# Moving three pieces of side work in a cached-attention training step: broadcast rows made earlier, a weight's transposes begun later, the last column sums put behind the attention rows

## The chip, the cores and the metric

The kernel runs on one core of one Trainium2 chip. The metric is the device time of an execution in microseconds (us). Executions of one kernel scatter by some 0.3%, so versions are compared on the same chip in alternating rounds. A ratio here is the mean time of one kernel's fast runs over that of the other's of the same rounds, so it is not quite the ratio of the medians that are quoted beside it. Times with two decimals such as 721.31 are read in a trace, counted from the start of its span.

## The reference, cut to what matters

```python
# x: 4 rows of 512; k_cache, v_cache: 4 x 32 heads x 4096 x 128 (bf16, 1 MB a head)
h   = x + attention(layernorm(x), k_cache, v_cache, wq, wo)
out = h + swiglu(layernorm(h), w1, w3, w2)
outputs: out, and the gradients to x, k_cache, v_cache, wq, wo, w1, w3, w2
```

There are 128 heads of 1 MB. The forward pass reads K and V once (256 MB). The backward pass reads V once more and writes one gradient of K and one of V per head: 3 MB a head, 384 MB. A head's 1 MB is 2^20 bytes, so these 640 MB are 671 of the 707.87 MB (of 10^6 bytes) that the profile counts; most of the rest are weights and their gradients.

## The kernel before

The forward pass forms, per head, P x K (`PK`), M = V' x PK on TensorE, and column sums of PK (`kP`). All arrays of a head live in 23 buffers of 1 MB. At the end of the forward pass come the attention rows, the norm and the MLP for four tokens, and from there dO, the gradient of the attention's output. Names that end in _ps or begin with pt_ are tiles that TensorE writes: al_ps takes the last attention rows, kt_ps the flushed sums, pt_hT the transposed rows for the norm, rb_ps the norm's mean and scale. A unit of wo is 8 transposes on TensorE and a copy.

```python
def M_end(s):                       # head s of the forward pass
    ...
    for c in range(2):
        for q in range(4):          # 8 matmuls: column sums of P x K into kP
            nc.tensor.matmul(hold["kP"][...], lhsT=ones_window(w), rhs=PK[...], ...)
    nc.scalar.copy(out=M_of(s), in_=hold["M"][:, 0:Dh + 1])
    PKs.pop(s).give(); Vs.pop(s).give()      # the buffers come free
# ... end of the forward pass
M_mm(NH - 1, 0, SJ); M_end(NH - 1)
O_cols(NH - MC, NH)
attn_page(2); attn_page(3)          # attention rows of the last pages
kP_flush(NH - 1)                    # ScalarE copy, 4 matmuls kt_ps, ScalarE copy
# ... norm, MLP, dO, first gv
```

The backward pass, per head: `V_T` transposes V (TensorE, evicted by ScalarE), 32 small matmuls make dP, which also frees V's buffer for a later load; VectorE writes the outer products gv (needs broadcast rows of dO) and gk (rows of q), and each goes out as one store of 1 MB.

```python
def front(s):
    if s % REP == 0:                # REP = 4: rows of dO and q for heads s..s+3
        replicate(s)                # 2 x (4 matmuls, ScalarE copy)
    V_T(s, psT)
    dP_ps = ...                     # 32 matmuls
    (vring if len(V2s) + len(VTs) + len(vring) < NV2 else free).append(sl.i)   # NV2 = 7

O0, S0 = 2, 21
for s in range(NH):
    prefetch()                      # loads of V into buffers of vring
    front(s + 1)
    grad_V(s + 1)                   # gv: VectorE, then its store
    grad_K(s)                       # gk
    if s >= S0:   step("s", 1 if s < S0 + 38 else 3)   # other gradients
    elif s >= O0: step("o")         # pages 1 to 3 of wo: transposes, then dO's columns and rows
```

## Time and profile before

| what | value |
|---|---|
| time, three runs | 1723.05 us median (1722.40 to 1723.24) |
| span of the profiled execution | 1719.8 us |
| bytes moved, mean rate | 707.87 MB, 412 GB/s |
| busy: TensorE, VectorE, ScalarE, GpSimd | 77%, 73%, 56%, 26% |
| busy: 16 DMA engines | 90% or more in 39 of 40 slices |

Read the row of DMA shares before the engines' shares. Where the transfers are busy from end to end, an engine's idle time has a price only if it leaves the transfers without work. The execution with this profile took 1721.68 us.

### The profile page before, as it was taken

To read this page: it belongs to the slowest core of one execution; us is meant where nothing else is said; L and a number is where in the kernel's file an instruction comes from. 1 tells how busy PE (TensorE), PEld (TensorE's weight loads), DVE (VectorE), ACT (ScalarE), POOL (GpSimd) and SP (SyncE) were. 2 spreads that over 40 slices of the span, in tenths; PEclk is the share of its full clock that TensorE was granted. 3 is DMA by queue.
4 is the path that set the end of the run, shared out by engine and by line. 5 is a ranking of instruction groups with operands and counts; after the bars stand their busy time and mean duration, and the time that the engine had idled before them with its cause. 6 is when DMAs were issued, how large, how long until landed. Compare 5 with 4: busy or idle time off the path is not lost.

```text
span 1719.8 us, 44279 instructions
## 1 busy us (share of the span) xinstructions
PE 1328.0 (77%) x19124; PEld 1124.5 (65%) x19124; DVE 1255.4 (73%) x1389; ACT 960.1 (56%) x1470; POOL 450.7 (26%) x808
## 2 busy tenths in 40 slices
PE   5888888888888888887787888767638777887771
PEld 4667666676666666876677877766536555665660
DVE  5989899889998997666667666766566566656582
ACT  3455444444454444677655555547537666766760
POOL 1211222222222231221233233322232332222221
PEclk9999999999999999666655555557765575555655
DMA  9999999999999999999999999999999999999997
GB/s 398 418 419 418 419 418 419 418 418 417 416 416 406 418 405 391 380 418 418 414 412 414 412 415 413 415 419 418 421 423 413 418 418 414 414 418 420 409 419 314
DMA packets 101867, 707.87 MB, mean 412 GB/s; under 512 B 11284, under 2 KB 15392, under 8 KB 17704
## 3 DMA queue, kind: packets, MB, share of 16 engines
q1 hardware_dynamic: 62272, 422.60, 59.4%
q0 software_dynamic: 39008, 282.37, 40.2%
q8 instruction: 150, 2.46, 0.6%
q14 instruction: 45, 0.37, 0.1%
q10 hardware_dynamic: 392, 0.07, 0.0%
HBM read 422.59 MB, written 282.34 MB: 410 GB/s over the span
## 4 chain that ended last, share of the span: by engine, by line
DMA 50%; PE 4%; DVE 3%; ACT 2%; issue 2%; POOL 0%; POOLq 0%; DVEq 0%; ACTq 0%
DMA out_dram<-gk 33%; DMA out_dram<-gv 15%; DMA out_dram<-gw 2%; ACT V L761 2%; DVE gk L766 1%; DVE gv L766 1%; PE pt_tps L760 1%; PE M_ps L433 1%; DVE PK L418 1%; PE pt_w L562 0%; PE gps L942 0%; ACT Pn L397 0%; PE kP_ps L443 0%; PE dP_ps L1148 0%; PE gu_ps L833 0%
## 5 line engine op out<-in xcount | busy, mean ns | idle before, releaser
L761 ACT COPY V<-pt_tps 128x1024 bf16<-128x1024 bf16 x512 | 492.5, 1016 | 192.0 <-PE pt_tps L760 131.8
L760 PE MATMUL pt_tps<-ident_b,V 128*128 128x128 bf16 x4096 | 453.2, 293 | 57.7 <-ACT V L761 53.7
L760 PEld LDWEIGHTS <-V 128*128 128x128 bf16 x4096 | 401.7, 138 | 122.3 <-issue 114.4
L766 DVE TENSOR_TENSOR gv<-P,reps 128x4096 bf16<-128x4096 bf16 x125 | 286.6, 2293 | 203.8 <-DMA out_dram<-gk 76.1
L766 DVE TENSOR_TENSOR gk<-dS,reps 128x4096 bf16<-128x4096 bf16 x128 | 293.4, 2292 | 108.5 <-DMA out_dram<-gv 54.3
L433 PE MATMUL M_ps<-PK,Vn 128*128 128x130 bf16 x4096 | 285.4, 222 | 50.6 <-DMA Vn<-in_A_v_cache_dram 50.2
L418 DVE TENSOR_TENSOR PK<-Kn,PK 128x4096 bf16<-128x4096 bf16 x128 | 292.3, 2284 | 32.3 <-POOL PK L414 32.0
L433 PEld LDWEIGHTS <-Vn 128*128 128x128 bf16 x4096 | 252.1, 99 | 72.0 <-DMA Vn<-in_A_v_cache_dram 66.3
L325 DVE STREAM_TRANSPOSE KT<-Kn 128x512 f32<-128x512 f32 (+1 forms) x321 | 250.7, 797 | 0.3 <-issue 0.2
L320 ACT COPY KT<-pt_tps 128x1024 bf16<-128x1024 bf16 x128 | 129.5, 1012 | 189.8 <-PE pt_tps L319 147.1
L1148 PE MATMUL dP_ps<-dOT_bf,V 128*128 128x1 bf16 x4096 | 145.4, 166 | 107.4 <-DVE dSt L1158 60.5
L1148 PEld LDWEIGHTS <-V 128*128 128x128 bf16 x4096 | 138.8, 104 | 122.4 <-issue 66.7
L1165 POOL DMA_DIRECT2D out_dram<-gk x128 | 68.2, 533 | 401.2 <-DMA out_dram<-gk 153.6
L331 POOL TENSOR_TENSOR W<-qrep,wmask 128x128 bf16<-128x128 bf16 x128 | 124.3, 971 | 81.8 <-PE S_ps L351 67.1
L414 POOL COPY PK<-P_all 128x64 bf16<-128x64 bf16 x128 | 32.6, 255 | 420.9 <-ACT P_all L408 417.8
L777 POOL DMA_DIRECT2D out_dram<-gv x128 | 68.4, 534 | 268.2 <-DMA out_dram<-gv 90.3
L1138 POOL COPY P<-P_all 128x64 bf16<-128x64 bf16 x125 | 127.4, 1019 | 0.0
L408 ACT COPY P_all<-pt_P 32x64 bf16<-32x64 bf16 x256 | 52.1, 203 | 59.5 <-PE pt_P L404 57.3
L319 PE MATMUL pt_tps<-ident_b,Kn 128*128 128x128 bf16 x1024 | 80.7, 223 | 0.0
L443 PE MATMUL kP_ps<-PK,onesw 128*32 128x512 bf16 x1024 | 79.2, 386 | 0.0
L319 PEld LDWEIGHTS <-Kn 128*128 128x128 bf16 x1024 | 62.1, 100 | 25.8 <-issue 25.8
L351 PE MATMUL S_ps<-KT,W 128*32 128x256 bf16 x1536 | 75.2, 285 | 0.5 <-DVE KT L325 0.2
(237 smaller groups left out, 1314.4 us busy)
## 6 DMA issues: line engine op xcount, KB each, us to landing
Kn<-in_A_k_cache_dram SPq DMA_DIRECT2D x128, 1024.0 KB, 15.6
Vn<-in_A_v_cache_dram SPq DMA_DIRECT2D x128, 1024.0 KB, 15.8
V<-in_A_v_cache_dram SPq DMA_DIRECT2D x128, 1024.0 KB, 10.9
out_dram<-gv POOLq DMA_DIRECT2D x128, 1024.0 KB, 27.4
out_dram<-gk POOLq DMA_DIRECT2D x128, 1024.0 KB, 27.3
wq<-in_A_wq_dram SPq DMA_DIRECT2D x8, 1024.0 KB, 10.3
out_dram<-gw POOLq DMA_DIRECT2D x6, 896.0 KB, 28.0
wo<-in_A_wo_dram SPq DMA_DIRECT2D x4, 1024.0 KB, 13.3
```

The source lines that it names most:

```text
L319: nc.tensor.transpose(pt[:, i, :], Kn[:, c * GW + i, :], ident_b[:])
L320: nc.scalar.copy(out=KT[:, c * GW:(c + 1) * GW, :], in_=pt[:])
L325: nc.vector.transpose(out=KT[:, c * w_:(c + n) * w_], in_=Kn[:, c * w_:(c + n) * w_])
L331: nc.gpsimd.tensor_tensor(out=W[:, hl], in0=qrep[:, :, s:s + 1].to_broadcast([P, 4, 32]), in1=wmask[:, hl, None, :].to_broadcast([P, 4, 32 ...
L418: nc.vector.tensor_tensor(out=PK[:, :, 0:Dh].rearrange("p j (r t) -> p j r t", t=2), in0=Ks[s].heads().rearrange("p j (r t) -> p j r t", t=2),
L433: nc.tensor.matmul(hold["M"][:], lhsT=Vn[:, j, :], rhs=PK[:, j, :], start=(j == 0), stop=(j == SJ - 1))
L443: nc.tensor.matmul(hold["kP"][32 * q:32 * (q + 1), :, :], lhsT=ones_window(w), rhs=PK[:, j0:j0 + 4, 0:Dh], start=(w == 0 and c == 0), stop ...
L760: nc.tensor.transpose(pt[:, i, :], v[:, g * GW + i, :], ident_b[:])
L761: nc.scalar.copy(out=v[:, g * GW:(g + 1) * GW, :], in_=pt[:])
L766: nc.vector.tensor_tensor(out=dst.rearrange("p j (r t) -> p j r t", t=2), in0=col2[:, :, None, :].to_broadcast([P, SJ, Dh // 2, 2]), in1=r ...
L1138: nc.gpsimd.tensor_copy(out=P2s[s][:], in_=P_all[:, s, :, None].to_broadcast([P, SJ, 2]))
L1148: nc.tensor.matmul(dP_ps[:, j:j + 1], lhsT=VT[:, j, :], rhs=dOT_bf[:, s:s + 1], start=True, stop=True)
```

## The change

Its intent: no wait for broadcast rows at the start of the backward pass, less side work for TensorE and ScalarE in its first heads, and a shorter way from the last head of the forward pass to the first store.

```diff
-    def M_end(s):
+    def kP_mm(s):                    # the 8 matmuls of the column sums
 ...
+        PKs.pop(s).give()
+
+    def M_end(s, kP=True):
+        if kP:
+            kP_mm(s)
 ...
-    M_end(NH - 1)
+    M_end(NH - 1, False)
 ...
     attn_page(3)
+    kP_mm(NH - 1)
     kP_flush(NH - 1)
 ...
-        woT(2, "s")                  # two units of wo before rb_ps
+        woT(1, "s")
 ...
         nc.tensor.matmul(rb_ps[:], lhsT=ones_f[0:B, :], rhs=rdiag[:], ...)
+        woT(1, "s")
 ...
-            if s % REP == 0:
-                replicate(s)
+            if s % REP == REP - 2 and s + 2 < NH:
+                replicate(s + 2)
 ...
-        O0, S0 = 2, 21
+        O0, S0 = 5, 24
 ...
-                step("s", 1 if s < S0 + 38 else 3)
+                step("s", 1 if s < S0 + 32 else 3)
```

More of the change, by code (lines that the diff above doesn't have):

```diff
@@ L447, in M_end @@
         nc.scalar.copy(out=M_of(s), in_=hold["M"][:, 0:Dh + 1])
-        PKs.pop(s).give()
         Vs.pop(s).give()
```

## The prediction

> **What bounds the kernel now.** I read the page's slices first, then the transfers' rate by stage, then the order of time around the few places where that rate is low.
>
> The row of DMA busy shares and the row of rates in the page (40 equal slices of the 1719.8 us span):
>
> ```profile
> DMA  9999999999999999999999999999999999999997
> GB/s 398 418 419 418 419 418 419 418 418 417 416 416 406 418 405 391 380 418 418 414 412 414 412 415 413 415 419 418 421 423 413 418 418 414 414 418 420 409 419 314
> ```
>
> The 16 DMA engines are busy in every slice, while no compute engine passes 77% (TensorE) over the span. The rate sits on a plateau of about 418 GB/s. The kernel moves 707.87 MB; at 418 GB/s this is 1693.5 us, so only 26 us of the span are not explained by bytes at the plateau. The table by stage says where they are (columns: stretch, its length, busy time and count of PE, PEld, DVE, ACT, POOL, then granted clock, DMA share, GB/s):
>
> ```profile
> 0.00:4.00 4.00, 0.00 (x0) 0.00 (x0) 0.84 (x6) 1.28 (x1) 2.76 (x17) 1.00 0.55 166
> 4.00:662.00 658.00, 547.35 (x9103) 449.26 (x9104) 588.81 (x795) 321.17 (x708) 164.87 (x384) 0.99 1.01 417
> 662.00:680.00 18.00, 16.21 (x241) 12.41 (x243) 10.29 (x10) 5.96 (x15) 2.23 (x3) 1.00 1.05 356
> 680.00:702.00 22.00, 20.84 (x395) 18.40 (x387) 10.81 (x34) 13.15 (x20) 0.58 (x3) 0.84 1.02 415
> 702.00:714.00 12.00, 10.44 (x148) 9.60 (x149) 9.09 (x16) 7.59 (x10) 4.47 (x7) 0.67 0.95 381
> 714.00:730.00 16.00, 12.36 (x188) 11.04 (x186) 11.15 (x9) 11.24 (x13) 4.04 (x7) 0.61 0.92 345
> 730.00:1702.00 972.00, 720.77 (x9061) 623.82 (x9059) 624.44 (x524) 599.72 (x706) 271.72 (x391) 0.60 1.01 416
> 1702.00:1719.80 17.80, 0.00 (x0) 0.00 (x0) 0.00 (x0) 0.00 (x0) 0.00 (x0) 0.50 0.40 169
> ```
>
> A stage loses length x (418 - rate) / 418: 2.4 us at the start, 1.6 in the forward pass, 2.7 in 662-680, 0.2 in 680-702, 1.1 in 702-714, 2.8 in 714-730, 4.7 in 730-1702, 10.6 in the drain: 26 in all. In 662-680 the engines are full (share 1.05); there the packets are short (wo arrives in 1 KB pieces: 2,408 of 2,546 packets in 662-672 are under 2 KB). The change touches neither the start, nor these packets, nor the bytes. What it can reach is the hand-over to the backward pass, 702-730: 1.1 + 2.8 = 3.9 us, or 0.23%.
>
> **What the Trainium skill says.** "DMA: Bandwidth & Descriptors", section "Where 436 GB/s comes from", puts the ceiling of the 16 ports at 435 GB/s; the plateau of 418 is 96% of it, so I take it as the wall. The same page, "Anatomy of one DMA", fits a transfer as 2.0 us plus bytes over 436 GB/s: 4.4 us for 1 MB. The trace has 4.7 us for the gv store issued at 717.95 with little beside it, which agrees, and 27.4 us for the median store: the rest is queueing behind other transfers. "Perfetto Trace Analysis", "Identifying the Most-Contended Engine", says to improve that engine first; here this is the transfers, and nothing in the diff shortens one.
>
> **Part 1: rows two heads ahead (and part 2, wo later).** Before, the broadcast rows of dO and q for heads 4 to 7 are made at the front of head 4, in TensorE's and ScalarE's way, behind the first wo unit. In order of time (start, length, what, idle before and who ended it; lines of other engines cut):
>
> ```profile
> 725.83 0.37 PE L1148 MATMUL dP_ps<-dOT_bf,V 128*128 128x1 bf16 x8 [0.49 <-ACT V L761]
> ...
> 726.06 1.01 PE L571 MATMUL pt_wo<-ident_b,wo 128*128 128x128 bf16 x8
> ...
> 727.12 1.01 ACT L215 COPY wo<-pt_wo 128x1024 bf16<-128x1024 bf16 x1 [1.34 <-PE pt_wo L571]
> 728.02 0.59 ACT L1129 CAST reps<-rep_ps 128x512 bf16<-128x512 f32 x1
> ...
> 728.70 2.29 DVE L766 TENSOR_TENSOR gv<-P,reps 128x4096 bf16<-128x4096 bf16 x1 [3.30 <-ACT reps L1129]
> ```
>
> VectorE stood 3.30 us for those rows. In the changed kernel they come at the front of head 2: gv(4) can follow gk(2) directly, 2.4 us earlier than 728.70, and gk(3), gv(5) likewise. The buffer it needs is free: only four output buffers rotate here, gv(4) takes that of gv(2), landed by 717.95 + 4.7 = 722.7.
>
> But the work only moves. Two sets of four small matmuls with ScalarE copies of 0.59 us take TensorE from 727.01 to 729.18, 2.2 us. Set before the transposes of head 2 (now at 715.69), they push dP(2) from 721.2 to 723.4 and dP(3) from 726.2 to 728.4. dP(2) releases the buffer for the load of V issued at 721.31, and dP(3) that at 726.27: both loads start 2.2 us later. gk(2), 723.11 before, slips by some 0.8 us. The third load (734.81) comes about 1.4 us earlier, because wo units cost heads 2 to 4 each about 0.9 us of TensorE and 1.01 us of ScalarE, which are now spent after head 5.
>
> What is this worth in transfers? From 714 to 721 only stores are in flight, and their times do not change (gk(0) issued 713.42, gv(2) 717.95, gk(1) 720.75): the 0.70 and 0.72 shares of 716-720, loss 1.2 us, stay. From 722 to 728 the share is already 0.93 to 1.07 with rates of 283 to 360, loss 1.4 us. There the late loads cost up to 0.5 us (one transfer fewer in flight around 722-724) and the stores that come 2.4 us sooner give back up to all of 1.4. I estimate a gain of 0.9, between 0 and 1.4. From 728 on the rate is 418 again and an earlier store only queues longer. The rows are also waited for at five later places (7.5, 7.5, 2.0, 11.5 and 6.3 us of VectorE, between 1306 and 1478). They will vanish, but the transfers run at 414 to 416 GB/s with share 1.01 there: worth nothing. Side work begins at head 24 instead of 21 but takes triple steps from 56 instead of 59, so its some 207 steps end at head 114 instead of 115: no change.
>
> **Part 3: the last column sums and the wo unit.** In order of time before:
>
> ```profile
> 679.81 0.62 PE L443 MATMUL kP_ps<-PK,onesw 128*32 128x512 bf16 x8
> ...
> 681.12 1.89 PE L478 MATMUL al_ps<-wo,OT_bf 128*4 128x512 bf16 x8
> ...
> 684.05 0.19 ACT L458 COPY kPT<-kt_ps 128x32 f32<-128x32 f32 x1 [2.99 <-PE kt_ps L457]
> 684.29 0.41 PE L806 MATMUL pt_hT<-ident_f,rows_t 4*128 4x4 f32 x4 [0.28 <-ACT kPT L458]
> ...
> 685.63 0.38 PE L820 MATMUL rb_ps<-rdiag,ones_f 4*128 4x8 f32 x2
> ```
>
> The eight sums (0.55 us net) leave their place before the attention rows, which end at 682.5 instead of 683.0. But the flush of the sums still stands before pt_hT in TensorE's order. Before, its ScalarE copy (0.59) lay beside the attention rows; now it cannot start before the sums, at 683.0: copy to 683.6, kt_ps (1.02) to 684.7, its copy to 685.0, pt_hT at 685.0 instead of 684.29. ScalarE's square root for the norm also queues behind that copy (684.85 becomes about 685.0). One wo unit (0.5 us) before rb_ps instead of two wins 0.5 back, the other fills the gap of 0.68 us before gu_ps. Net, rb_ps at about 685.9 instead of 685.63: I expect the first store of gv to come 0.2 us LATER, not earlier. As 702-714 waits on it, this costs 0.2.
>
> **Sum.** 1723.05 - 0.9 + 0.2 = 1722.35; I go to 1722.0, since the late waits on rows that vanish may give the transfers a little in the 414 GB/s stretches.
>
> **Rivals.** (a) The hand-over closes wholly: -3.9, so about 1719. For it: the 3.30 us wait stands exactly in the low-rate stretch. Against: half of the loss lies before 722, on stores that the change does not move. (b) Held buffers starve the stores: pages 1 to 3 of wo keep their three buffers three heads longer, so four outputs rotate to head 10 instead of 7. With four, 760-840 ran at 417 GB/s and share 1.01 (four rising to six), so I give it nothing; were the share there 0.95 for three heads of 7.5 us, it would cost 1.1 us: 1723.5. (c) The path before the first gv grows by 0.7 us, pt_hT's whole slip: 1722.9. (d) The drain: 10.6 us of loss after 1702 depend on how evenly the last stores (3.0 MB are left at 1702) lie over the 16 engines; shifts upstream can move it by 2 us either way, unrelated to the intent.
>
> **Range and chances.** The mechanisms span about -3.9 to +1.8; with the drain's scatter and the 0.8 us between the three runs, 1717.5 to 1726.0 should hold it. A change of 2% is 34 us; all loss that is not bytes is 26, so faster by 2% is nearly excluded. Slower by 2% needs a starved backward pass, for which the trace gives no sign.
>
> **What would show it.** Right: bytes and plateau unchanged; no wait of gv on the rows; loads of V issued near 723.5 and 728.4 by this clock; pt_hT near 685.0; 714-730 at 350 to 385 GB/s instead of 345. Wrong: 730-850 under 410 GB/s or share under 0.98 (buffers starve, b); 716-720 filled (a); gv(0) issued earlier than 707.79 (part 3 misread); a drain of much over or under 18 us (d).

## The result, and the profile after

The changed kernel took 1725.80 us median (1724.54 to 1728.72, six runs) against 1723.14 (1722.40 to 1724.24, six runs): ratio 1.0016, 95% interval 1.0003 to 1.0029. This lies in the stated range and within 2%, but on the other side of zero from the point that was forecast. Two later comparisons, on chips 14 and 5, gave 1.0003 (0.9989 to 1.0017) and 1.0002 (0.9989 to 1.0015).

The table by stage of the kernel after, with the columns of the prediction's table:

```profile
662.00:680.00 18.00, 16.19 (x255) 12.35 (x246) 10.94 (x10) 5.87 (x14) 2.49 (x4) 1.00 1.06 363
680.00:702.00 22.00, 20.63 (x369) 17.81 (x367) 10.48 (x32) 13.00 (x19) 0.50 (x3) 0.84 1.02 415
702.00:714.00 12.00, 9.82 (x185) 9.10 (x183) 8.69 (x17) 6.54 (x9) 3.05 (x5) 0.85 0.90 358
714.00:730.00 16.00, 13.08 (x190) 11.75 (x188) 13.20 (x12) 11.35 (x13) 9.34 (x11) 0.58 0.95 371
730.00:1702.00 972.00, 733.61 (x9070) 637.12 (x9066) 623.09 (x522) 600.86 (x707) 270.12 (x391) 0.58 1.01 416
1702.00:1723.40 21.40, 0.00 (x0) 0.00 (x0) 0.00 (x0) 0.00 (x0) 0.00 (x0) 0.50 0.34 144
```

Apart from 662-680 (363 GB/s instead of 356, ahead of the change), three rows differ from before. 702-714 fell from 381 to 358 GB/s: the first store of gv comes later. Its issue before,

```profile
707.79 0.63 POOL L777 DMA_DIRECT2D out_dram<-gv  x1 [3.88 <-DVE dOT_bf L735]
```

and after:

```profile
709.35 0.63 POOL L782 DMA_DIRECT2D out_dram<-gv  x1 [3.82 <-DVE dOT_bf L740]
```

714-730 rose from 345 to 371, as forecast, though mostly for another reason than the one forecast (see the point on the late loads below). And the drain after 1702, when only stores are left, is 3.6 us longer, at 144 GB/s instead of 169.

The chain of instructions at the end of the forward pass, in order of time (start, length, engine and instruction; other rows cut):

```profile
681.60 1.46 PE L482 MATMUL al_ps<-wo,OT_bf 128*4 128x512 bf16 x6
...
682.68 0.40 PE L443 MATMUL kP_ps<-PK,onesw 128*32 128x512 bf16 x3
682.89 0.38 PE L482 MATMUL al_ps<-wo,OT_bf 128*4 128x512 bf16 x1
...
683.11 0.38 PE L482 MATMUL al_ps<-wo,OT_bf 128*4 128x512 bf16 x1
...
683.98 0.58 ACT L458 COPY kP_sb<-kP_ps 128x512 f32<-128x512 f32 x1 [2.87 <-PE al_ps L482]
...
685.97 0.41 PE L811 MATMUL pt_hT<-ident_f,rows_t 4*128 4x4 f32 x4 [0.28 <-ACT kPT L462]
...
687.15 0.59 PE L825 MATMUL rb_ps<-rdiag,ones_f 4*128 4x8 f32 x2
```

The sums' copy on ScalarE (683.98), which lay beside the attention rows before, now follows them and holds up pt_hT. The sums' matmuls also slip in ahead of the last two of the attention rows, although they stand behind them in the program; all five traces with the sums moved show the same order.

The heads 2 to 4 of the backward pass, in order of time:

```profile
716.92 0.60 PE L1132 MATMUL rep_ps<-dOrows_bf,ident_b 32*128 32x128 bf16 x4
...
722.60 0.83 PE L1154 MATMUL dP_ps<-dOT_bf,V 128*128 128x1 bf16 x24
...
724.88 2.29 DVE L771 TENSOR_TENSOR gk<-dS,reps 128x4096 bf16<-128x4096 bf16 x1
...
727.08 2.29 DVE L771 TENSOR_TENSOR gv<-P,reps 128x4096 bf16<-128x4096 bf16 x1
```

gv(4) starts at 727.08 directly after gk(2), with no wait on rows; before, it started at 728.70 after a wait of 3.30 us. No wait of gv on the rows' copy is left anywhere in the trace; before there were six, 38.1 us in all. But dP(2), which starts at 722.60, releases the first load of V. The load queue before,

```profile
721.31 0.33 SPq L793 DMA_DIRECT2D V<-in_A_v_cache_dram  x1
...
726.27 0.33 SPq L793 DMA_DIRECT2D V<-in_A_v_cache_dram  x1
```

and after:

```profile
724.37 0.33 SPq L798 DMA_DIRECT2D V<-in_A_v_cache_dram  x1
...
729.72 0.33 SPq L798 DMA_DIRECT2D V<-in_A_v_cache_dram  x1
```

Both loads start 3.1 to 3.5 us later. Of this 0.9 us is the forward pass, which ran that much later in this execution (the last block of M began at 678.77 instead of 677.84, in code that the change does not touch); the rest, 2.1 to 2.5 us, is the change, about the 2.2 us of the prediction. There is a stretch of low rate behind them. In windows of 2 us of the kernel after:

```profile
732.00:734.00 2.00, 1.76 (x35) 1.61 (x32) 2.00 (x2) 1.81 (x3) 1.18 (x2) 0.50 1.00 360
734.00:736.00 2.00, 1.75 (x23) 1.75 (x24) 1.14 (x3) 0.61 (x2) 1.36 (x2) 0.50 0.98 279
```

Before, the same two windows ran at 442 and 410 GB/s, while 724-728 ran at 283 and 328. The DMA engines count as busy there; it is the packets that take longer. The transfers of the last of these windows by queue (packets, MB, share of the 16 engines):

```profile
q1 hardware_dynamic: 63, 0.52, 93.1%
```

93.1% of 16 engines for 2 us is 29.8 us, or 473 ns for each of 63 load packets, with hardly a store beside them. In the traces a packet of 8 KB in the stores of the drain takes 309 ns (median). But loads that run alone are not slow as such. In the same trace the stores were slow at 726-728 (453 ns each), and at 728-730 the loads ran just as alone at 317 ns each and 389 GB/s. The queue of the stores in the first of these windows and that of the loads in the second:

```profile
q0 software_dynamic: 61, 0.40, 86.3%
...
q1 hardware_dynamic: 94, 0.77, 93.0%
```

Why packets take longer in some of these windows stays open.

### The profile page after: what moved, and what is told of

The parts are those of the page before. It is cut to its first block, busy times and chain, and to the rows that moved or that the text cites. A ratio compares the mean times of both kernels' runs of the same rounds, so it can differ in the third digit from the quotient of the medians.

```text
span 1723.4 us, 44279 instructions
## 1 busy us (share of the span) xinstructions
PE 1341.0 (78%) x19124; PEld 1138.7 (66%) x19124; DVE 1255.3 (73%) x1389; ACT 959.7 (56%) x1470; POOL 450.9 (26%) x808
## 4 chain that ended last, share of the span: by engine, by line
DMA 48%; PE 4%; DVE 4%; ACT 3%; issue 2%; POOL 1%; POOLq 0%; DVEq 0%; ACTq 0%
DMA out_dram<-gk 34%; DMA out_dram<-gv 12%; DVE gk L771 2%; ACT V L766 2%; DMA out_dram<-gw 1%; DVE gv L771 1%; PE pt_tps L765 1%; PE M_ps L433 1%; DVE PK L418 1%; PE gps L948 0%; POOL P L1144 0%; PE pt_w L566 0%; ACT Pn L397 0%; PE dP_ps L1154 0%; PE kP_ps L443 0%
## 5 line engine op out<-in xcount | busy, mean ns | idle before, releaser
L765 PE MATMUL pt_tps<-ident_b,V 128*128 128x128 bf16 x4096 | 460.6, 296 | 58.8 <-ACT V L766 54.3
L765 PEld LDWEIGHTS <-V 128*128 128x128 bf16 x4096 | 408.5, 140 | 131.7 <-issue 123.8
L771 DVE TENSOR_TENSOR gv<-P,reps 128x4096 bf16<-128x4096 bf16 x125 | 286.6, 2293 | 200.1 <-DMA out_dram<-gk 92.3
L418 DVE TENSOR_TENSOR PK<-Kn,PK 128x4096 bf16<-128x4096 bf16 x128 | 292.3, 2284 | 33.4 <-POOL PK L414 33.1
L1154 PEld LDWEIGHTS <-V 128*128 128x128 bf16 x4096 | 139.5, 104 | 109.7 <-ACT V L766 59.7
L397 ACT ACTIVATE Pn<-E,rl 128x1024 bf16<-128x1024 f32 x64 | 73.7, 1152 | 3.2 <-DVE rl L394 3.2
```

The source lines that it names most:

```text
L418: nc.vector.tensor_tensor(out=PK[:, :, 0:Dh].rearrange("p j (r t) -> p j r t", t=2), in0=Ks[s].heads().rearrange("p j (r t) -> p j r t", t=2),
L765: nc.tensor.transpose(pt[:, i, :], v[:, g * GW + i, :], ident_b[:])
L771: nc.vector.tensor_tensor(out=dst.rearrange("p j (r t) -> p j r t", t=2), in0=col2[:, :, None, :].to_broadcast([P, SJ, Dh // 2, 2]), in1=r ...
L1154: nc.tensor.matmul(dP_ps[:, j:j + 1], lhsT=VT[:, j, :], rhs=dOT_bf[:, s:s + 1], start=True, stop=True)
```

## The experiments

Twelve runs were made: the changed kernel twice more (e1, e8) and ten other kernels. Bytes moved up to a moment are worked out from the trace of each; with transfers never short of work, 0.42 MB are 1 us.

**The change once more (e1) and a third time (e8).** No edit.

> The changed kernel once more, beside its parts on the same chip. It measured 1.0016 of before. All theories: 1.0010 to 1.0025 again, about +2.7 us. Its trace tells whether the late end of the transfers repeats: in the first trace 21.4 us after 1702 at 144 GB/s, against 17.8 us at 169 GB/s before. Theory T (the loss is in the hand-over, through the longer path to the first gv): 702-714 again near 358 GB/s and gv(0) about 1.5 us later than before. Rival D (the end of the run is uneven over the DMA engines, which has nothing to do with the intent): the stretches up to 1702 are level with before and the extra time lies after it.

> The changed kernel a third time, since the first comparison gave 1.0016 (1.0003 to 1.0029) and the second 1.0003 (0.9989 to 1.0017). If there is a real loss: 1.0005 to 1.0015. If the first was chance: 0.9993 to 1.0008. Bytes moved at 1690 us again 699.8 to 700.0 MB, as in every trace so far; what differs is the thinning of the engines after that.

Measured: e1 1724.42 us median against 1724.17 of before (ratio 1.0003, 0.9989 to 1.0017); e8 1723.96 against 1724.78 (1.0002, 0.9989 to 1.0015). At 702-714 e1 ran at 367 GB/s, and its drain was long again (21.5 us after 1702). In e8 699.60 MB had moved at 1690 us, under the 699.8 that were forecast. The loss of the first comparison did not repeat: 0.3 to 0.5 us in place of 2.7, none of it told from zero.

**Each part alone.**

```diff
 e2: +            if s % REP == REP - 2 and s + 2 < NH: replicate(s + 2)
 e3: +        O0, S0 = 5, 24        (and S0 + 32)
 e4: +    kP_mm(NH - 1) behind attn_page(3);  woT(1) on both sides of rb_ps
```

> Only the rows of dO and q two heads ahead; wo from head 2 and the sums as before. Prediction's step: -0.9 us (0 to -1.4), ratio 0.9992 to 1.0000. Rival B (held wo buffers cost): exactly before, 1.0000, as wo is not touched. Rival D: anything within 2 us of before, and no relation to 714-730 in its trace.

> Only pages 1 to 3 of wo begun at head 5 instead of 2, side work at 24 instead of 21. Theory T: -0.5 to 0 us. Rival B (three buffers held three heads longer starve the stores): +2 to +3 us, ratio 1.0012 to 1.0018, nearly the whole loss, and a rate under 410 GB/s between 750 and 850. Rival D: within 2 us either way, rates up to 1700 as before.

> Only the last column sums behind the attention rows and one of two wo units moved behind rb_ps. Prediction's step: +0.2 us; the trace of the changed kernel shows the way from the last M to the first gv longer by 0.63 us, so theory T now says +0.6 us, ratio 1.0003. If the hand-over carried the whole loss it would be +2.7 us, 1.0016. Rival B: 1.0000.

Measured against the same runs of before (1724.17 us median): e2 1723.50, ratio 0.9997 (0.9984 to 1.0009); e3 1724.01, 1.0003 (0.9991 to 1.0016); e4 1724.24, 1.0004 (0.9991 to 1.0016). None is told from zero. The interval of e3 still allows the smaller losses that rival B named, but its trace shows no starving: from 760 to 900 us, with the buffers held, it moved 58.4 MB (before: 58.0). In the trace of e2 alone the loss in 714-730 even grew (316 GB/s): of the 0.45 MB missing against before, 0.34 are missing at 726-730. The first load had come at 723.29 and the wo units still delayed the heads after it; that these are the cause is not shown.

**A dose of delay (e5, e6).** Does a microsecond that the transfers lose in the hand-over cost a microsecond at the end? I doubted it after seeing how unevenly the 16 engines finish.

```diff
+        for _ in range(16):          # e6: 48
+            nc.vector.tensor_copy(out=u[:], in_=u[:])
         nc.vector.tensor_tensor(out=dhT[:], in0=u[:], in1=grT[:], op=ALU.add)
```

> The kernel before with 16 copies of u onto itself put into VectorE's chain just before dO's rows, so that the first gv and all stores after it come some 3.3 us later (16 x 0.21 us, the step between such operations in the trace). A dose of the loss that the change was to remove. Theory T (time lost by the transfers in the hand-over is lost at the end): 730 us into the span about 1.3 MB behind before (300.35 MB), and +3.3 us at the end, ratio 1.0019. Theory S (the end is set by the one or two DMA engines that lag; the gap is a gap of those that run ahead, and is made up later): as far behind at 730, but the difference shrinks by 1118, and the end moves by 0 to 1.5 us, ratio 1.0000 to 1.0009.

> The same with 48 copies, 10 us. Theory T: +10 us, ratio 1.0058, and 4 MB behind at 730 as well as at 1690. Theory S: more than the lag of the slow engines can hide, so a part shows: +6 to +8 us, ratio 1.0035 to 1.0046. If even this vanishes, something after the hand-over has slack that neither theory names.

Measured: e5 1727.77 us against 1724.78, ratio 1.0018 (1.0005 to 1.0030), about 3.1 us; e6 1733.77, ratio 1.0056 (1.0043 to 1.0068), about 9.7 us. Counted from the start of the last head's block of M, the first gv was issued after 33.20 and 38.10 us, against 29.92 (mean of before, e2, e3 and e7; with e9, e10 and e11, whose way is unchanged too, it is 29.98, from 29.43 to 30.62): delays of 3.3 and 8.2 us, within the intervals of what the end moved. The bytes moved up to 1690 us in e6 (line of all transfers):

```profile
DMA packets 100264, 696.25 MB, mean 412 GB/s; under 512 B 11098, under 2 KB 15206, under 8 KB 17518
```

Before had 699.87 MB at that moment and e5 698.46. At 730 us the two were 1.18 and 2.77 MB behind before (300.35), at 1690 us 1.41 and 3.62 MB (e6's hand-over was not over at 730; at 760 us it was 3.38 behind). What is missed in the hand-over is never made up; theory S falls. So the hand-over was worth attacking, and the question is why the change won nothing there.

**Rows and wo without the sums (e7).**

> The rows two heads ahead and wo from head 5, without the change to the sums and the unit before rb_ps: the prediction's gain without its cost. Theory T: first gv as before, 714-730 at 370 GB/s or more, -0.9 us, ratio 0.9995. Theory S: the same better rate in 714-730, and nothing at the end: 0.9990 to 1.0010.

Measured: 1725.10 us against 1724.78, ratio 1.0006 (0.9993 to 1.0020), and 349 GB/s in 714-730, so the forecast of 370 missed. The first load came at 723.83. Its slow stretch was 724-728 (246 and 319 GB/s); at 732-736, where the changed kernel fell to 360 and 279, it ran at 393 and 430. So loads this late do not alone make that second dip, which all three traces of the changed kernel have.

**Rows made after dP instead of before the transposes (e9).** The test of what e7 pointed to.

```diff
 def front(s):
-    if s % REP == REP - 2 and s + 2 < NH:
-        replicate(s + 2)
     V_T(s, psT)
     ... dP ...
     (vring if ... else free).append(sl.i)
+    if s % REP == REP - 2 and s + 2 < NH:
+        replicate(s + 2)
```

> Rows and wo as in e7, but in each front the rows are made after the dP matmuls instead of before the transposes, so that dP(2), and with it the first load of V in the backward pass, is not put off. The theory under test: the gain of the earlier stores was eaten because the loads of V start 2.0 to 3.1 us later and their slow stretch (packets of 470 ns instead of 309 while one load runs nearly alone) only moved from 722-728 to 726-736. Then here: first load at 721 to 722 by the clock of before (plus up to 0.9 us that the forward pass ran later), bytes at 760 us 0.2 to 0.5 MB above e7 at equal start, end -0.5 to -1.2 us against before, ratio 0.9993 to 0.9997. Rival: the order does not matter, as TensorE has the same work up to dP(3): bytes at 760 as e7 and ratio 1.0000 to 1.0006.

Measured: the first load at 721.07, and by stage for e7

```profile
714.00:730.00 16.00, 13.07 (x193) 11.80 (x192) 12.92 (x12) 11.15 (x13) 6.38 (x9) 0.60 0.91 349
```

and for e9

```profile
714.00:730.00 16.00, 12.51 (x194) 11.33 (x192) 14.34 (x12) 11.88 (x14) 5.97 (x9) 0.71 0.93 367
```

| kernel | MB in 714-730 | MB in 730-740 | both | MB up to 760 |
|---|---|---|---|---|
| before | 5.51 | 4.23 | 9.74 | 312.94 |
| changed, three traces | 5.93, 5.89, 5.99 | 3.83, 3.83, 3.67 | 9.76, 9.72, 9.66 | 312.81, 312.87, 312.40 |
| e7 | 5.58 | 4.20 | 9.78 | 312.90 |
| e9 | 5.87 | 4.14 | 10.01 | 313.23 |

The changed kernel gains 0.4 MB in 714-730 and gives 0.4 MB back in 730-740. In e7, whose loads are late as well, both windows stay as before. With the loads left in their place e9 is 0.33 MB ahead of e7 at 760 us, 0.8 us of transfers. But the start was not equal, as the expectation asked: e9's last block of M began at 677.86 and e7's at 678.40, and 0.10 of the 0.33 MB were there at 714 already, so the order of the rows is worth 0.5 to 0.8 us. Nor did the loads alone move: the store issued at 726.92 in e7 came at 725.59 in e9, 0.8 us earlier beyond the start. And each is one trace, while the three of the changed kernel lie 0.47 MB apart at 760 us. So that the late loads ate the gain is likely, not shown. The time of e9, 1724.22 against 1724.78 of before (ratio 0.9997, 0.9983 to 1.0010), agrees and does not prove it. At 1690 us its trace was only 0.05 MB ahead of before; the eleven traces without added delay up to e11 lie between 699.47 and 700.00 MB there, so the stage from 760 to 1690 scatters by as much as this gain.

**Eight buffers for V (e10 on the kernel before, e11 on e7).**

```diff
-    NV2 = 7
+    NV2 = 8
```

> The kernel before with eight buffers kept for V in the backward pass instead of seven (NV2 = 8): the buffer of head 1 goes back to the loads, so the first load starts at dP(1), near 715.8, in the gap of 716-720, and three outputs rotate instead of four until wo page 1 is free. If the hand-over's loss is a want of transfers to run, 714-730 moves 0.4 to 0.9 MB more and the end is 1.0 to 2.0 us earlier: ratio 0.9988 to 0.9994. Rival: the stores, with one buffer less, wait for their landing and the loss only moves behind 730: 1.0000 to 1.0010.

> Rows two heads ahead and wo from head 5, with eight V buffers. First load at dP(1), before the rows are made, so the rows no longer put the first load off. If both remedies act on different parts of the loss: 1.5 to 2.5 us earlier than before, ratio 0.9985 to 0.9991, better than e10. If three outputs until head 10 are too few: 1.0005 or more.

Measured: e10 1724.15 us, ratio 0.9998 (0.9984 to 1.0011); e11 1724.82, ratio 1.0000 (0.9987 to 1.0014). The first load came earlier, at 717.41 and 715.63, but the stores now waited: in e11 the fifth was issued at 723.67 (before: 720.75). In 714-730 e10 moved 0.25 MB more than before (0.4 to 0.9 were forecast) and e11 0.03. In e11 the low rates (270 to 283 GB/s) lie at 722-728, over 6 us behind its first load, so a late load is not needed for them. This is the rival named for e10. Neither beats the kernel before.

**The sums alone (e12).** As e4, with both wo units left before rb_ps; one look.

> Only the last column sums behind the attention rows; both wo units stay before rb_ps. One look, for the lengths of the way from the last block of M in the trace, not for the time (its effect is under the scatter). Before: pt_hT +6.45, rb_ps +7.79, first gv +29.95 us after that block began. With sums and unit moved (e4): +7.49, +8.48, +30.43. If the flush of the sums is what lengthens the way, pt_hT is again at +7.2 to +7.5 here, and rb_ps, now behind two units, at +8.5 to +9.0, later than in e4; the first gv at +30.5 to +31.0. If the split unit were the cause: pt_hT +6.4 and the first gv +30.0.

Measured, from the start of the last block of M:

| trace | pt_hT | rb_ps | first gv issued |
|---|---|---|---|
| before | +6.45 | +7.79 | +29.95 |
| e4, sums and unit | +7.49 | +8.48 | +30.43 |
| e12, sums only | +7.21 | +8.54 | +31.47 |

The flush of the sums is what lengthens the way, as the prediction said. Splitting the wo units wins 0.06 us back at rb_ps in e4 and 0.16 to 0.45 in the three traces of the changed kernel (+8.38, +8.09, +8.09). From rb_ps to the first gv the time goes with TensorE's granted clock in that stretch: 22.8 to 23.0 us in the three traces with 0.70 of full speed (e8, e10, e12), 22.0 to 22.3 in the eight with 0.77 or 0.78, 21.65 in e11 with 0.84. The kernel e10 does not move the sums and had 0.70 too, so e12's +31.47, later than its forecast of 30.5 to 31.0, is partly this clock.

## Why the prediction was right or wrong, point by point

**The bound and the size of what could be won: right.** Bytes and plateau are unchanged, and no version moved the end by more than 0.2% save the added delays. E5 and e6 show the sum's basis, that time lost by the transfers in the hand-over is lost at the end.

**Part 1, the stores come earlier: right; its worth is likely and not shown.** The wait on rows is gone and gv(4) follows gk(2). Where the loads kept their place (e9, with wo later as well) the transfers were 0.29 MB, 0.7 us, ahead of before at 760 us, from the same start; the estimate was 0.9. This is one trace of each, and less than the scatter named above. The five later waits on rows vanished and brought nothing that is seen: VectorE's idle time before gv was 203.8 us in all before and 200.1 after, now spent on waits for stores to land.

**Part 1, the net of late loads and early stores: this step failed.** The prediction said that the late loads "cost up to 0.5 us" and that from 728 on the rate is 418 again. The loads came as late as it said (723.4 and 728.8 with the 0.9 us of the forward pass taken off). But the gain that was to be 0.9 us is 0.04 MB, 0.1 us, in e7, which has this part and not the sums (9.78 MB in 714-740 against 9.74 before). In the changed kernel 732-736 is slow instead. The cost of the late loads measures 0.5 to 0.8 us (e7 against e9, with the limits said there) in place of up to 0.5, most or all of the gain. The mechanism by which packets slow down stays open. The check named for this step, 714-730 at 350 to 385 GB/s, came true at 371 by luck. Of the 0.42 MB gained there 0.37 lie in 716-720, which the prediction held fixed: the first stores, issued 1.6 us later, fall into it. Without the sums (e7) it was 349, and the window ended before the loss did.

**Part 3: direction right, size too small.** It was to cost 0.2 us. pt_hT came 0.75 us later by this clock (the prediction said 0.7). rb_ps came 0.3 to 0.6 later in the three traces of the changed kernel (0.27 was said), and the first gv after +30.58, +30.13 and +31.10 us, with e4 +30.43: on average 0.64 us more than 29.92, or 0.58 more than the mean of all seven unchanged ways, which themselves reach 30.62. Two things were missed: the sums' matmuls ran between the last attention rows, so in the changed kernel the last of these was added 0.45 us earlier and not 0.5 (in e4 0.16); and rb_ps itself was on average 0.47 us late in these four traces. These 0.47 us, from 0.30 to 0.69, are what the change costs here. The rest is mostly the third trace, which took 23.0 us from rb_ps to the first gv at the lower granted clock of 0.70, where the others took 22.0 to 22.2. Whether moving the sums makes that clock likelier (two of five traces with it, one of seven without) is not shown.

**The sum.** With these terms, -0.7 + (0.5 to 0.8) + (0.5 to 0.6) is an estimate of +0.3 to +0.7 us in place of -0.7. The three comparisons of the changed kernel, 1.0016, 1.0003 and 1.0002, average to +1.2 us, with intervals of some 2 us either way for each; together, not told from zero either.

**Rivals.** (a), the hand-over closes wholly: no; 716-720 rose to 422 and 352 GB/s but at the cost of 702-714, where the first stores now arrive later. (b), held buffers: the trace of e3 shows no shortage. (c), a longer way to the first gv: right, at 0.5 to 0.6 us. (d), the drain: right that it is the largest single scatter. The drain before, in windows of 4 us,

```profile
1710.00:1714.00 4.00, 0.00 (x0) 0.00 (x0) 0.00 (x0) 0.00 (x0) 0.00 (x0) 0.50 0.36 154
1714.00:1718.00 4.00, 0.00 (x0) 0.00 (x0) 0.00 (x0) 0.00 (x0) 0.00 (x0) 0.50 0.06 25
```

and after:

```profile
1710.00:1714.00 4.00, 0.00 (x0) 0.00 (x0) 0.00 (x0) 0.00 (x0) 0.00 (x0) 0.50 0.21 88
1714.00:1718.00 4.00, 0.00 (x0) 0.00 (x0) 0.00 (x0) 0.00 (x0) 0.00 (x0) 0.50 0.13 53
1718.00:1722.00 4.00, 0.00 (x0) 0.00 (x0) 0.00 (x0) 0.00 (x0) 0.00 (x0) 0.50 0.02 10
```

A DMA share of 0.13 is two of 16 engines, 0.02 a third of one: at the end one or two engines finish what they have left while the others are done. At 1690 us the two kernels had moved 699.87 and 699.84 MB, the same within 0.1 us. So in these two traces the whole difference of 3.6 us in span arises after 1690. The remaining 8 MB took 29.8 us before and 33.4 after; in e1 to e4 and e7 to e11 they took 32.2 to 34.4 us, whichever part of the change was in. Before has only this one profile, of a run shorter than its usual ones. Its later runs had spans of 1722.0 and 1722.5 us (medians), 1720.0 at the least, where the profiled one had 1719.8, and e1 and e8 had 1722.3 and 1721.9 beside them. So the profile of before is of an unusually short execution; that its drain is usually longer is likely, but no trace shows it. This stays open, and with it whether the first comparison's 1.0016 was chance or a loss of up to 2 us that only its chip shows.

## What to carry to other kernels

Where the transfers are the bound, ask of every moved instruction which transfer it releases: work that is pulled forward to serve a store can put off a load by as much, and a gap closed in one window opens in the next. Judge such a change by bytes moved up to a moment well behind the place, in several traces, not by the rate in the window that it aimed at. A difference of 2 us in 1720 needs several comparisons and several profiles; one trace of each kernel differed by 3.6 us in its last 30 us alone, while the two kernels, timed again, were 0.3 to 0.5 us apart.

## What the Trainium skill lacked or had wrong

- "DMA: Bandwidth & Descriptors", "Anatomy of one DMA", fits a transfer that GpSimd issues as 2.0 us plus bytes over 436 GB/s. It fits a lone store here, which GpSimd issues too (4.4 us for 1 MB by the fit, 4.7 measured), but the page has no word on loads that start while the store queue runs empty: packets took 453 ns (stores) in the window 726-728 of the changed kernel and 473 ns (loads) in 734-736, against 309 ns for an 8 KB packet in the drain, though loads took only 317 ns in 728-730.
- The same page says of lagging engines only that two of the 16, 7 and 15, are usually slower. It has nothing on how unevenly the 16 end a long stream of equal transfers: from 1704 to 1706 us on ever fewer engines ran, in the end one or two, in both traces shown here (10.6 us of lost transfer time before, 14.0 in the first trace after). Which engines lag, the traces do not tell.
- "TensorE: Matmul & The Clock Gate" names a reorder window in "Back-to-back issue gap", for pairs of weight load and matmul, and says in "The mechanism" that matmuls themselves start in program order. Here later matmuls started before earlier ones: three kP_ps matmuls began at 682.68, ahead of the last two al_ps at 682.89 and 683.11, which stand before them in the program (the program puts the sums at four column positions of the array and these rows at one). All five traces with the sums moved show it.
- Nothing wrong was found in "HBM Reference": it says that a core streaming alone measures about 425 GB/s; the plateau of 418 agrees.
